# Loads of q, k and v moved from GpSimd's DMA queue to SyncE's, with the casts, the tails and the order of work changed along

## The chip, the cores and the metric

The kernel runs on one core of one Trainium2 chip. The metric is the device time of one execution in microseconds. A core has TensorE (PE, with its weight loads as PEld), VectorE (DVE), ScalarE (ACT), GpSimd (POOL) and SyncE (SP), and 16 DMA engines[...].

## What is computed

Linear attention with a feature map, then a two-layer block on its output. Batch and heads are 8 and 8, a sequence has 576 positions, a head 64 elements; the inner width is 2048.

```python
def phi(x):
    proj = np.einsum('bhsd,df->bhsf', x, w_phi)              # 64 -> 128
    proj = proj - np.max(np.abs(proj), axis=-1, keepdims=True)
    return np.concatenate([np.exp(proj), np.exp(-proj)], axis=-1)
q_p, k_p = phi(q), phi(k)
kv  = np.einsum('bhsf,bhsd->bhfd', k_p, v)
z   = np.sum(k_p, axis=2)
num = np.einsum('bhsf,bhfd->bhsd', q_p, kv)
den = np.einsum('bhsf,bhf->bhs', q_p, z)[..., None] + 1e-06
x   = (num / den), heads side by side: 4608 tokens x 512
h = x @ w_in                                                 # 512 -> 2048
g = np.where(h > 0, h, np.exp(np.minimum(h, 0)) - 1)
out = g @ w_out                                              # 2048 -> 512
```

## The kernel before

Attention works on quads: four heads of one batch, so 16 quads. Of 576 positions of a head, 512 are the main part (four rows of 128, `NT`), 64 the tail. The tails of the four heads are packed into one tile of 128 partitions: heads 0 and 2 on partitions 0 to 63, heads 1 and 3 on 64 to 127 (s is the half, c the pair).

Steps of a quad, each a function in `attention_steps`:

- `transposes`: TensorE transposes k and q (L166, tails L174), DVE copies them from PSUM to `kT`, `qT`.
- `k_head` (four heads and the tail): a projection `pk` (L195), a reduction for the largest absolute value `m_k` on DVE (L202), two exponentials `EK` on ACT (L215).
- `k_scale`: `em` on ACT (L223), then POOL scales v by it into `vs` (L229) and, for the tails, into `vst` (L240), a tile with zeros for the other half.
- `q_head`: projection and reduction `m_q`. `q_features`: projection `pq` (L250) and exponentials `Eq` (L258), tails `Eqt` (L273), and `w` (L280).
- `kv`: TensorE sums `EK` times `vs` (L299) and the tails (L288) into `pkv`; ACT copies it to `kv`.
- `out_head` and `out_tail`: `Eq` times `kv` gives `pn` (L322, tails L344), DVE weights and adds them into `tot` and `tott`; column 64 is the denominator.
- `divide`: `den` and `rec` on DVE (L367, L372, L373), `x` on POOL (L376, tails `xt` L382).
- `x_out`: TensorE transposes `x` (L393), DVE copies it into `xT` of its batch, and the tails into `xT_tail`.

The second block (called MoE in the code) works on chunks of 512 tokens: eight chunks of main rows, one per batch, and one of all tails. `mm1` is one of 16 first-stage units of a chunk: four matmuls `ph` (L438), `e_sb` on ACT (L446), `u_sb` on POOL (L448), `gT` on DVE (L451). `mm2` is one of four second-stage units: 16 matmuls `po` (L459), a copy `o_sb` on ACT (L467), a DMA out. 180 units in all. Their PSUM tiles come from a pool of four, those of attention from another four.

The loop over n runs 17 slots. Slot n does kv, out and x of quad n-1 mixed with k, scale and q of quad n, and the transposes of quad n+1 at its end. After slots 2, 4, ... the units of the batch just finished are put into `pending`, and the next two slots put them between their steps: none in slots 0 to 2, eight per slot in 3 and 4, ten per slot from 5 to 16; 44 are left for the end.

Loads: k and q of a quad by POOL's software queue with a cast to bf16 (L136), tails of a whole batch by six DMAs on the same queue (L108), weights and w_phi there too (L84, L91, L72, L73); v in fp32 by SP (L145), where the outputs are issued as well (L470). [...]the framework that builds the program may hoist an instruction ahead of others of its queue where its inputs allow. [...]

Of the kernel before, what the change touches and what calls it, by code (L numbers as in the profile page):

```python
# [12 lines left out]
ACT = mybir.ActivationFunctionType  # L13

# [7 lines left out]
def kernel(  # L22
# [11 lines left out]
    P = 128  # L34
# [11 lines left out]
    N_CHUNK = NTOK // CHUNK  # L46
    NT = 4
    MAIN = NT * P
    TAIL = S - MAIN
    NQ = 2 * B  # L50
    D1 = D + 1

    consts = ctx.enter_context(tc.tile_pool(name="consts", bufs=1))
    loads = ctx.enter_context(tc.tile_pool(name="loads", bufs=3))
    work = ctx.enter_context(tc.tile_pool(name="work", bufs=2))
    small = ctx.enter_context(tc.tile_pool(name="small", bufs=4))
    xtp = ctx.enter_context(tc.tile_pool(name="xtp", bufs=3))
# [10 lines left out]
    make_identity(nc, ident)  # L68

    w_phi_both = consts.tile([P, 2, F], BF16)  # L70
    nc.vector.memset(w_phi_both, 0.0)
    nc.gpsimd.dma_start(out=w_phi_both[0:D, 0, :], in_=w_phi)  # L72
    nc.gpsimd.dma_start(out=w_phi_both[D:P, 1, :], in_=w_phi)  # L73
# [7 lines left out]
    def load_w_in():  # L81
        for ct in range(N_CT):
            for c in range(2):
                nc.gpsimd.dma_start(  # L84
                    out=w_in_sb[c * D:(c + 1) * D, ct, :],
                    in_=w_in_r[ct // 2, c, ct % 2],
                )

    def load_w_out():
        for jt in range(0, N_JT, 4):  # L90
            nc.gpsimd.dma_start(  # L91
                out=w_out_sb[:, jt:jt + 4, :], in_=w_out_r[:, jt:jt + 4, :]
            )
# [5 lines left out]
    q_tails = consts.tile([P, NQ, 2, D], BF16)  # L99
    k_tails = consts.tile([P, NQ, 2, D], BF16)  # L100
    v_tails = consts.tile([P, NQ, 2, D1], BF16)
    nc.vector.memset(v_tails[:, :, :, D:D1], 1.0)

    def load_tails(b):
        for src, dst in ((k, k_tails), (q, q_tails), (v, v_tails)):
            heads = src[b].rearrange("(gc s) j d -> s j gc d", s=2)
            for s in range(2):
                nc.gpsimd.dma_start(  # L108
                    out=dst[s * TAIL:(s + 1) * TAIL, 2 * b:2 * b + 2, :, 0:D].rearrange(
                        "p g c d -> p (g c) d"  # L110
                    ),
                    in_=heads[s, MAIN:S],
                )


    NV = 3
    v_bufs = []
    for i in range(NV):
        vb = consts.tile([P, 4, NT, D1], FP32, name=f"v_main{i}")
        nc.vector.memset(vb[:, :, :, D:D1], 1.0)  # L120
        v_bufs.append(vb)

    vst_bufs = []
    for i in range(2):
        t = consts.tile([P, 2, 2, 2, D1], BF16, name=f"vst{i}")
        nc.vector.memset(t, 0.0)
        vst_bufs.append(t)

    qk_loaded = {}

    def load_quad(i):
        b, qd = divmod(i, 2)
        got = []
        for src, nm in ((k, "k_main"), (q, "q_main")):
            t = loads.tile([P, 4, NT * D], BF16, name=nm)
            nc.gpsimd.dma_start(  # L136
                out=t,
                in_=src[b, 4 * qd:4 * qd + 4, 0:MAIN, :].rearrange(
                    "h (p t) d -> p h (t d)", t=NT
                ),  # L140
            )
            got.append(t)
        vb = v_bufs[i % NV]
        for hh in range(4):
            nc.sync.dma_start(  # L145
                out=vb[:, hh, :, 0:D],
                in_=v[b, 4 * qd + hh, 0:MAIN, :].rearrange(
                    "(p t) d -> p t d", t=NT
                ),
            )  # L150
        qk_loaded[i] = (got[0], got[1], vb)


    def attention_steps(i):
# [3 lines left out]
        def transposes():  # L158
            k_main, q_main, _ = qk_loaded[i]
            kT = work.tile([P, 9, P], BF16, name="kT")  # L160
            qT = work.tile([P, 9, P], BF16, name="qT")
            for src, dst in ((k_main, kT), (q_main, qT)):
                tr = apsum.tile([P, 8, P], BF16, name="tr", tag="ap")
                for hh in range(4):
                    for tp in range(2):
                        nc.tensor.transpose(  # L166
                            tr[:, 2 * hh + tp, :],
                            src[:, hh, tp * P:(tp + 1) * P],
                            ident,
                        )  # L170
                nc.vector.tensor_copy(dst[:, 0:8, :], tr)  # L171
            trt = apsum.tile([P, 2, P], BF16, name="trt", tag="ap")
            for n, (src, dst) in enumerate(((k_tails, kT), (q_tails, qT))):
                nc.tensor.transpose(  # L174
                    trt[:, n, :],
                    src[:, i, :, :].rearrange("p c d -> p (c d)"),
                    ident,
                )
            nc.vector.tensor_copy(kT[:, 8, :], trt[:, 0, :])
            nc.vector.tensor_copy(qT[:, 8, :], trt[:, 1, :])  # L180
            st["kT"], st["qT"] = kT, qT
            st["m_k"] = small.tile([P, 18], FP32, name="m_k")
            st["m_q"] = small.tile([P, 18], FP32, name="m_q")
            st["EK"] = work.tile([P, 4, 2, NT * F], BF16, name="EK")
            st["EKt"] = work.tile([P, 2, 2 * F], BF16, name="EKt")
            st["Eq"] = work.tile([P, 2, 2, 2, 4 * P], BF16, name="Eq")
            st["Eqt"] = work.tile([P, 2, 2 * P], BF16, name="Eqt")

        def project(xT, hh, m):
# [4 lines left out]
            for j in range(n):  # L194
                nc.tensor.matmul(  # L195
                    pk[:, 2 * j:2 * j + 2, :].rearrange("p a b -> p (a b)"),
                    xT[:, 2 * hh + j, :],
                    w_phi_rhs,
                    start=True,
                    stop=True,  # L200
                )
            nc.vector.tensor_reduce(  # L202
                m[:, 4 * hh:4 * hh + 2 * n],
# [16 lines left out]
        def k_scale():  # L220
            em = small.tile([P, 2, 18], FP32, name="em")
            for sg in range(2):
                nc.scalar.activation(  # L223
                    em[:, sg, :], st["m_k"], ACT.Exp, scale=2.0 * sg - 1.0
                )
            vb = qk_loaded[i][2]
            vs = work.tile([P, 4, 2, NT, D1], BF16, name="vs")
            for hh in range(4):
                nc.gpsimd.tensor_tensor(  # L229
                    vs[:, hh],  # L230
                    vb[:, hh:hh + 1].to_broadcast((P, 2, NT, D1)),
                    em[:, :, 4 * hh:4 * hh + 4, None].to_broadcast(
                        (P, 2, NT, D1)
                    ),
                    op=ALU.mult,
                )
            vst = vst_bufs[i % 2]
            for s in range(2):
                r = slice(s * TAIL, (s + 1) * TAIL)
                nc.gpsimd.tensor_tensor(  # L240
                    vst[r, :, :, s, :],
                    v_tails[r, i:i + 1].to_broadcast((TAIL, 2, 2, D1)),
                    em[r, :, 16:18, None].to_broadcast((TAIL, 2, 2, D1)),
                    op=ALU.mult,
                )
            st["vs"], st["vst"] = vs, vst
# [15 lines left out]
        def q_features_tail():  # L262
# [16 lines left out]
            w = small.tile([P, 18], FP32, name="w")  # L279
# [3 lines left out]
        def kv(c):  # L283
            if c == 0:
                st["kv"] = work.tile([P, 2, 2, 2, D1], BF16, name="kv")
            pkv = apsum.tile([P, 2, 2, D1], FP32, name="pkv", tag="ap")
            for sg in range(2):
                nc.tensor.matmul(  # L288
                    pkv[:, :, sg, :],
                    st["EKt"][:, sg, c * F:(c + 1) * F],  # L290
                    st["vst"][:, sg, c, :, :],
                    start=(sg == 0),
                    stop=False,
                    skip_group_check=True,
                )
            for s in range(2):
                for sg in range(2):
                    for t in range(NT):
                        nc.tensor.matmul(  # L299
                            pkv[:, s, sg, :],  # L300
                            st["EK"][:, 2 * c + s, sg, t * F:(t + 1) * F],
                            st["vs"][:, 2 * c + s, sg, t, :],
                            start=False,
                            stop=(t == NT - 1),
                            skip_group_check=True,
                        )
            nc.scalar.copy(st["kv"][:, c], pkv)

        def out_head(hh):
            c, s = divmod(hh, 2)  # L310
            if hh == 0:
                st["tot"] = work.tile([P, 4, NT, D1], FP32, name="tot", bufs=1)
                st["tott"] = work.tile([P, 2, D1], FP32, name="tott")
                st["x"] = work.tile([P, 2, NT, 2, D], BF16, name="x")
                st["xt"] = work.tile([P, 2, D], BF16, name="xt")
            pn = []
            for sg in range(2):
                pt = apsum.tile([P, NT, D1], FP32, name=f"pn{sg}", tag="ap")
                for t in range(NT):
# [5 lines left out]
                        st["kv"][:, c, s, sg, :],  # L325
# [4 lines left out]
            tot = st["tot"][:, hh]  # L330
# [3 lines left out]
                st["w"][:, 4 * hh:4 * hh + 4, None].to_broadcast((P, NT, D1)),  # L334
# [4 lines left out]
        def out_tail():  # L339
            pn = []  # L340
            for sg in range(2):
                pt = apsum.tile([P, 2, 2, D1], FP32, name=f"pn{sg}", tag="ap")
# [245 lines left out]
```

## Time and profile before

| | |
|---|---|
| median of 3 runs | 508.6 us (507.23 to 509.34) |
| the profiled execution | 507.1 us, span 505.3 us, mean granted clock 0.922 |
| PE busy | 409.6 us (81%) |
| PEld | 223.1 us (44%) |
| DVE | 306.1 us (61%) |
| ACT | 268.3 us (53%) |
| POOL | 278.5 us (55%), DMA issues counted in |
| DMA | 32.55 MB, mean 64 GB/s; software queue 14.19 MB, hardware queue 17.83 MB |
| chain that ended last | PE 52%, POOL 20%, DVE 13%, DMA 6% |

Busy time is a sum over the span; the stages differ, so the views by time below count for more. The span is what the profile sees, the execution's own time 1.8 us more. Rows of groups read: line, engine, operation, output and inputs, shapes, count, then busy us and mean ns of one, then idle time of the engine before them and who ended it.

### The profile page before, as it was taken

Reading aid. Unit: us, or ns where it says so; the run is one execution under the profiler, and the core shown is the slowest. Engines: PE = TensorE matmul, PEld = TensorE weight load, DVE = VectorE, ACT = ScalarE, POOL = GpSimd, SP = SyncE. Lnnn points to the kernel's source line nnn. Section 1 sums busy time; section 2 is a strip of 40 time slices with the busy share of each in tenths; the row PEclk is TensorE's granted clock in tenths of the full one; section 3 lists DMA queues with packets and bytes.
Section 4 is the critical chain, followed back from the end, with each engine's and each line's share of the span. In section 5 each row is a group of like instructions: output and inputs, shape, how many; then the busy total and the mean of one; then the engine's idle time right before and its main releaser. Section 6 shows DMA issues by size and latency. Waiting matters only on the chain.

```text
span 505.3 us, 8410 instructions
## 1 busy us (share of the span) xinstructions
PE 409.6 (81%) x3070; PEld 223.1 (44%) x3120; DVE 306.1 (61%) x647; ACT 268.3 (53%) x581; POOL 278.5 (55%) x420
## 2 busy tenths in 40 slices
PE   2573727495979797979797979797979798999996
PEld 1251415252635364536363546354545354444442
DVE  2562826886857677766777577757775855334420
ACT  1742608292847474847484748474847462444431
POOL 8669799747473737373737383818281734333310
PEclk9965959797989899989999999999998999899999
DMA  9999948231323232324242424200000000110113
GB/s 157 212 181 198 116 61 76 47 43 43 44 63 64 62 64 64 64 64 64 64 64 62 64 65 64 62 22 21 22 23 23 21 22 22 42 43 21 43 52 72
DMA packets 71944, 32.55 MB, mean 64 GB/s; under 512 B 48352, under 2 KB 66784, under 8 KB 71904
## 3 DMA queue, kind: packets, MB, share of 16 engines
q0 software_dynamic: 32864, 14.19, 23.1%
q1 hardware_dynamic: 39040, 17.83, 13.2%
q8 instruction: 24, 0.39, 0.3%
q14 instruction: 16, 0.13, 0.1%
HBM read 36.77 MB, written 9.44 MB: 91 GB/s over the span
## 4 chain that ended last, share of the span: by engine, by line
PE 52%; POOL 20%; DVE 13%; DMA 6%; issue 4%; ACT 4%; POOLq 0%; ACTq 0%
PE po L459 22%; PE ph L438 13%; POOL x L376 7%; DMA q_main<-in_q_dram 5%; POOL vs L229 4%; DVE m_q L202 4%; PE pq L250 4%; PE pn L322 3%; PE pkv L299 2%; POOL vst L240 2%; PE pk L195 2%; ACT EK L215 2%; POOL u_sb L448 2%; PE tr L166 2%; DVE den L367 2%
## 5 line engine op out<-in xcount | busy, mean ns | idle before, releaser
L448 POOL TENSOR_SCALAR u_sb<-e_sb 128x512 bf16<-128x512 f32 x144 | 88.9, 623 | 134.9 <-ACT e_sb L446 129.5
L459 PE MATMUL po<-w_out_sb,gT 128*128 128x512 bf16 x559 | 148.1, 389 | 1.8 <-DVE gT L451 1.4
L451 DVE SCALAR_TENSOR_TENSOR gT<-u_sb,ph 128x512 bf16<-128x512 bf16 x144 | 97.9, 683 | 78.9 <-POOL u_sb L448 78.1
L438 PE MATMUL ph<-xT,w_in_sb 128*128 128x512 bf16 x480 | 131.0, 390 | 4.6 <-DVE gT L451 3.4
L446 ACT ACTIVATE e_sb<-ph 128x512 f32<-128x512 f32 x144 | 87.3, 611 | 48.8 <-PE ph L438 46.8
L258 ACT ACTIVATE Eq<-pq 128x512 bf16<-128x512 f32 x128 | 65.2, 616 | 54.7 <-PE pq L250 54.7
L459 PEld LDWEIGHTS <-gT 128*128 128x128 bf16 x576 | 54.4, 100 | 50.5 <-issue 4.6
L438 PEld LDWEIGHTS <-w_in_sb 128*128 128x128 bf16 x576 | 54.6, 100 | 49.6 <-issue 6.8
L215 ACT ACTIVATE EK<-pk 128x512 bf16<-128x512 f32 x128 | 69.4, 612 | 13.1 <-DVE m_k L202 13.0
L229 POOL TENSOR_TENSOR vs<-v_main,em 128x520 bf16<-128x520 f32 x64 | 65.7, 1063 | 17.9 <-ACT em L223 17.7
L202 DVE TENSOR_REDUCE m_k<-pk 128x4 f32<-128x512 f32 (+1 forms) x80 | 50.4, 632 | 25.9 <-PE pk L195 25.6
L467 ACT COPY o_sb<-po 128x512 f32<-128x512 f32 x36 | 21.2, 589 | 68.0 <-PE po L459 67.5
L393 PE MATMUL tr<-ident,x 128*128 128x128 bf16 x128 | 14.6, 248 | 52.7 <-POOL x L376 52.7
L202 DVE TENSOR_REDUCE m_q<-pk 128x4 f32<-128x512 f32 (+1 forms) x80 | 48.5, 628 | 1.3 <-PE pk L195 0.5
L322 PEld LDWEIGHTS <-Eq 128*128 128x128 bf16 x512 | 28.9, 98 | 24.9 <-issue 17.0
L376 POOL TENSOR_TENSOR x<-tot,rec 128x256 bf16<-128x256 f32 x64 | 37.2, 614 | 3.1 <-DVE rec L373 3.0
L393 PEld LDWEIGHTS <-x 128*128 128x128 bf16 x128 | 8.4, 108 | 68.8 <-POOL x L376 68.8
L322 PE MATMUL pn<-kv,Eq 128*128 128x65 bf16 x512 | 34.0, 194 | 3.8 <-ACT EK L215 2.6
L195 PE MATMUL pk<-w_phi_both,qT 128*128 128x256 bf16 x144 | 29.6, 292 | 8.4 <-DVE m_q L202 7.0
L136 POOL DMA_DIRECT2D k_main<-in_k_dram x16 | 12.8, 802 | 35.9 <-PE tr L166 25.3
L195 PE MATMUL pk<-w_phi_both,kT 128*128 128x256 bf16 x144 | 29.6, 284 | 3.3 <-ACT EK L215 1.0
L171 DVE COPY kT<-tr 128x1024 bf16<-128x1024 bf16 x16 | 11.1, 692 | 34.1 <-PE tr L166 34.1
(61 smaller groups left out, 462.2 us busy)
## 6 DMA issues: line engine op xcount, KB each, us to landing
v_main<-in_v_dram SPq DMA_DIRECT2D x64, 128.0 KB, 3.3
out_dram<-o_sb SPq DMA_DIRECT2D x32, 256.0 KB, 2.6
k_main<-in_k_dram POOLq DMA_DIRECT2D x16, 256.0 KB, 5.3
q_main<-in_q_dram POOLq DMA_DIRECT2D x16, 256.0 KB, 5.7
w_in_sb<-in_moe_w_in_dram POOLq DMA_DIRECT2D x8, 256.0 KB, 10.2
w_out_sb<-in_moe_w_out_dram POOLq DMA_DIRECT2D x4, 512.0 KB, 8.3
out_dram<-o_sb SPq DMA_DIRECT2D x8, 128.0 KB, 2.3
k_tails<-in_k_dram POOLq DMA_DIRECT2D x16, 32.0 KB, 2.8
```

Source lines behind the costliest of these rows:

```text
L195: nc.tensor.matmul(pk[:, 2 * j:2 * j + 2, :].rearrange("p a b -> p (a b)"), xT[:, 2 * hh + j, :], w_phi_rhs, start=True, stop=True,)
L202: nc.vector.tensor_reduce(m[:, 4 * hh:4 * hh + 2 * n], pk[:, 0:2 * n, :], axis=AX.X, op=ALU.max, apply_absolute_value=True,)
L215: nc.scalar.activation(dst, pk, ACT.Exp, scale=1.0 - 2.0 * sg)
L229: nc.gpsimd.tensor_tensor(vs[:, hh], vb[:, hh:hh + 1].to_broadcast((P, 2, NT, D1)), em[:, :, 4 * hh:4 * hh + 4, None].to_broadcast((P, 2, ...
L258: nc.scalar.activation(st["Eq"][:, par, c, sg, :], pq, ACT.Exp, scale=1.0 - 2.0 * sg)
L322: nc.tensor.matmul(pt[:, t, :], st["Eq"][:, par, c, sg, o:o + P], st["kv"][:, c, s, sg, :], start=True, stop=True,)
L376: nc.gpsimd.tensor_tensor(st["x"][:, s, :, c, :], st["tot"][:, hh, :, 0:D], rec[:, 4 * hh:4 * hh + 4, None].to_broadcast((P, NT, D)), op=A ...
L438: nc.tensor.matmul(ph, w_in_sb[:, ct, jt * P:(jt + 1) * P], xTs[ch][:, ct, :], start=(ct == 0), stop=(ct == N_CT - 1),)
L446: nc.scalar.activation(e_sb, ph, ACT.Exp)
L448: nc.gpsimd.tensor_scalar(u_sb, e_sb, -1.0, 1.0, op0=ALU.add, op1=ALU.mult)
L451: nc.vector.scalar_tensor_tensor(gTs[ch][:, jt, :], u_sb, 0.0, ph, op0=ALU.min, op1=ALU.max)
L459: nc.tensor.matmul(po, gT[:, jt, tt * P:(tt + 1) * P], w_out_sb[:, jt, :], start=(jt == 0), stop=(jt == N_JT - 1),)
```

## The change

- k, q and v, tails included, are loaded by SP in fp32: four DMAs for k, four for q, six for v per quad. k and q land in staging tiles of 1152 columns (`k_st`, `q_st`, two of each), the last 128 columns hold the tails. POOL casts each in two pieces into `k_bf`, `q_bf`.
- Each quad's positions are nine columns per pair c (eight of two heads and one of tails), so `vs`, `tot`, `x`, `m`, `w`, `den` hold main part and tails in one tile; `vst`, `tott`, `xt` are gone. `vs` is four POOL instructions of 585 elements, `x` two of 576.
- The tail's matmuls read only their own 64 rows (`kv`: 64 rows of weights and of `vs`) or write only their own 64 (`out_tail`: 64 columns of weights). `kv(s)` takes the heads of one half s instead of a pair c.
- POOL's software queue carries weights alone, one issue after every second step of slots 0 and 1, `w_out` in eight DMAs for four. w_phi comes by SP and is cast by DVE.
- Slot 2 does kv, out and x of quad 1 first, then the keys and queries of quad 2. From there units are placed by an even rate, 136 of them over 14.4 slots; a second-stage unit follows after four first-stage ones. x comes after three q heads instead of five; scale comes after the tail's out and divide.
- `o_sb` has two buffers for four, `xT` two for three.

The core of the diff:

```diff
-        for src, nm in ((k, "k_main"), (q, "q_main")):
-            t = loads.tile([P, 4, NT * D], BF16, name=nm)
-            nc.gpsimd.dma_start(out=t, in_=...)
+        for src, nm in ((k, "k_st"), (q, "q_st")):
+            t = stage.tile([P, QW + P], FP32, name=nm)
+            heads = src[b, 4 * qd:4 * qd + 4]
+            for hh in range(0, 4, 2):
+                nc.sync.dma_start(out=t[:, hh * NT * D:(hh + 2) * NT * D]..., in_=heads[hh:hh + 2, 0:MAIN, :]...)
+            for s in range(2):
+                nc.sync.dma_start(out=t[s * TAIL:(s + 1) * TAIL, QW:]..., in_=...[s, MAIN:S])
...
+        def cast(n):
+            nm = ("k_bf", "q_bf")[n]
+            t = st[nm] = work.tile([P, QW + P], BF16, name=nm)
+            src = loaded[i][n]
+            for lo, hi in ((0, QW // 2), (QW // 2, QW + P)):
+                nc.gpsimd.tensor_copy(t[:, lo:hi], src[:, lo:hi])
...
+            for c in range(2):
+                for sg in range(2):
+                    r = slice(c * NS, (c + 1) * NS)
+                    nc.gpsimd.tensor_tensor(vs[:, sg, r, :], vb[:, r, :], em[:, sg, r, None]..., op=ALU.mult)
...
+            r = slice(s * TAIL, (s + 1) * TAIL)
+            for c in range(2):
+                for sg in range(2):
+                    nc.tensor.matmul(pkv[:, c, sg, :], st["EKt"][r, sg, c * F:(c + 1) * F],
+                                     st["vs"][r, sg, c * NS + 8, :], start=False, ...)
...
+                        o = c * P + s * TAIL
+                        nc.tensor.matmul(pt[r, sg, c, :], st["Eqt"][:, sg, o:o + TAIL], st["kv"][:, s, c, sg, :], ...)
...
+        if nxt:
+            steps += nxt["cast"]
+        if n == 2:
+            steps += old["kv"] + old["out"] + old["x"]
+            steps.append(lambda: chunk_ready(0))
+            steps += new["k"] + new["scale"] + new["q"] + new["qf"] + nxt["tr"]
+            return steps
...
+            if weights and n < 2 and j % 2 == 1:
+                weights.pop(0)()
+            due = (n + (j + 1) / len(steps) - 2.6) * 136 / 14.4
+            while done < due and (first or second):
+                moe_unit()
+                done += 1
...
+        if n + 2 < NQ:
+            load_qk(n + 2)
+            load_v(n + 2)
```

## The prediction, made before the changed kernel ran

> **What bounds the kernel now.** I read the slices of the page first (each digit is the busy tenth of 12.6 us):
>
> ```profile
> PE   2573727495979797979797979797979798999996
> ...
> POOL 8669799747473737373737383818281734333310
> PEclk9965959797989899989999999999998999899999
> DMA  9999948231323232324242424200000000110113
> ```
>
> The first twelve slices (152 us) differ from the rest: TensorE is mostly idle, POOL (GpSimd) is nearly full, its granted clock (PEclk) dips with the idle stretches, and the DMA engines are full for five slices only. The timeline of POOL alone shows with what:
>
> ```profile
> 56.65 1.23 POOL L108 DMA_DIRECT2D k_tails<-in_k_dram  x2
> 57.85 1.26 POOL L108 DMA_DIRECT2D q_tails<-in_q_dram  x2
> 59.06 1.28 POOL L108 DMA_DIRECT2D v_tails<-in_v_dram  x2
> 60.26 1.30 POOL L108 DMA_DIRECT2D k_tails<-in_k_dram  x2
> 61.82 1.24 POOL L108 DMA_DIRECT2D q_tails<-in_q_dram  x2 [0.26 <-issue]
> 63.03 1.25 POOL L108 DMA_DIRECT2D v_tails<-in_v_dram  x2
> ...
> 64.86 4.14 POOL L229 TENSOR_TENSOR vs<-v_main,em 128x520 bf16<-128x520 f32 x4
> 68.92 1.36 POOL L240 TENSOR_TENSOR vst<-v_tails,em 64x260 bf16<-64x260 bf16 x2
> ...
> 70.96 2.32 POOL L376 TENSOR_TENSOR x<-tot,rec 128x256 bf16<-128x256 f32 x4
> ```
>
> From 56.65 to 64.86 POOL only issues DMAs of tails, most for later batches, while the keys of quad 2 wait to be scaled: `vs` of that quad starts at 64.86 and `x` of quad 1 at 70.96. TensorE needs this `x` to start the first MoE chunk. So POOL's queue, not TensorE, sets the first 97 us. Later, the table by windows (time, then busy us of PE, PEld, DVE, ACT, POOL, then granted clock, DMA share, GB/s) shows one stretch of about a slot per line:
>
> ```profile
> 76.00:101.00 25.00, 15.59 (x143) 9.30 (x145) 19.31 (x37) 13.63 (x34) 21.71 (x34) 0.84 0.56 61
> 101.00:126.00 25.00, 18.01 (x155) 10.27 (x157) 18.83 (x42) 14.56 (x35) 14.36 (x21) 0.85 0.27 43
> ...
> 202.00:227.00 25.00, 22.24 (x180) 12.23 (x181) 18.23 (x39) 15.62 (x35) 14.40 (x21) 0.96 0.31 64
> ```
>
> A slot with ten MoE units takes 25.6 us (x to x: from 169.95 to 426.15 in ten slots), one with eight 24.1 (120.46 to 144.58). By matmul pitch (0.2157 us for 512 columns, from 3.45 us for 16 in the chain of waits) the same slots need 20.8 and 17.5 us. So a slot is not TensorE's alone: 3.3 us more matmul costs 1.5 us. What fills the difference is in the waits (us in total, times, longest) and the groups:
>
> ```profile
> POOL u_sb L448 <- ACT e_sb L446: 129.5, 88, 5.1
> ...
> PE tr L393 <- POOL x L376: 52.7, 27, 9.7
> ```
>
> ```profile
> L448 POOL TENSOR_SCALAR u_sb<-e_sb 128x512 bf16<-128x512 f32 x144 | 88.9, 623 | 134.9 <-ACT e_sb L446 129.5 <-DVE tot L331 3.9
> ...
> L229 POOL TENSOR_TENSOR vs<-v_main,em 128x520 bf16<-128x520 f32 x64 | 65.7, 1063 | 17.9 <-ACT em L223 17.7
> ...
> L376 POOL TENSOR_TENSOR x<-tot,rec 128x256 bf16<-128x256 f32 x64 | 37.2, 614 | 3.1 <-DVE rec L373 3.0
> ...
> L108 POOL DMA_DIRECT2D k_tails<-in_k_dram x16 | 10.2, 654 | 0.0
> ```
>
> After the em of a slot, POOL runs vs (4.1), vst (1.3), one or two u_sb (0.62 each) and x (2.3) in this order, about 8.3 us, and PE waits for x at the end of it, 2.4 us per slot in the steady part.
>
> [...]
>
> **The change part by part**, for the profiled execution (span 505.3, its run 507.1; so I add 1.8 to a span, and 1.5 more for the median of 508.6).
>
> *POOL.* Removed: k, q and w_phi issues 12.8 + 12.1 + 1.1, tails 30.5, vst 19.9, xt 6.4. vs becomes 64 of 585 elements at 2.04 ns, 1.20 each, 76.5 (was 65.7); x 32 of 576, by the two rows 614 for 256 and 397 for 128 (1.70 ns each + 180) 1.16 each, 37.0 (was 37.2). Added: 64 casts, 512 or 640 fp32 to bf16, by L448 0.62 and 0.78, 2.8 per quad, 44.9[...]; w_out in 8 issues for 4, +2.4. Sum 278.5 to about 254; per slot the part from em to x falls from 8.3 to 4.8 + 0.6 + 2.3 = 7.7.
>
> *SP.* 14 loads per quad for 4, at 0.54 us (L145's shortest): 7.6 us of a slot, no bound. [...]outputs stand behind them, but land in 2.6 us and are read by nobody. Loads of quad i+2 wait for the cast of quad i, two slots ahead of their own cast, so in the steady part casts find data. DMA engines: k and q are written in fp32, 2 x 4.7 MB more; hidden later (share 0.3), not in the first 60 us.
>
> *Start.* (1) Quad 0's loads issue from SP in 8 x 0.54 and land by 7.5, w_phi by 8.5; two small DVE copies (0.21 each, by L179) make it bf16: the first projection at 9 for 11.5. (2) Quad 1's loads wait behind v(0) until about 10 and land at 16; POOL's casts of quad 1 stand ahead of vs(0), so vs(0) runs 18 to 23 for 20.97 to 26.3: 3 us gained of what the issues cost. (3) In slot 1 x(0) comes after the last w_out issues[...]: x(0) at 36 for 44.6, vs(1) until 43. (4) Slot 2 does batch 0's kv, out and x first: 43 + 9 = 52 by durations; the casts of quads 3 and 4 stand ahead of x(1) on POOL and need 5 quads and all weights, 12.5 MB written; the kernel before moved at most 212 GB/s, so 59 if nothing gets faster with fp32 rows, 52 if it does. I take 57, for 70.96. (5) Slot 2's keys now come after x instead of beside: + 8.5 to em, + 4.8 vs: kv(2) at 70 for 79.5. So x(2) is at 86 for 96.84. **Start: -10.5** (-17 to 0).
>
> *Slots x(2) to x(15).* 329.3 us for 13 now. By instruction order the matmuls there fall from 259 to 257 us, since 136 units are spread evenly instead of eight then ten: by the slope of one half -1. The part from em to x -0.6 per slot, DVE's tail work (tott, two den) -0.8 beside others, taken as -0.2. x stands two q heads earlier in PE's order: 3.7 us of matmul cover it after the tail for 5.0, so PE idles longer, but the moved work fills the stretch before the next kv, which is TensorE's: 0. Casts follow x, while ACT is in its 4.03 us of Eq and u_sb waits for e_sb anyway (129.5 us of such waits): 0; their cost uncovered is the rival below. [...] Eight more small matmuls per quad (65 columns, 0.0325 each) replace eight of 130 at 0.06: 0. Sum 13 x (-0.8 + 0.3) - 1 = **-7.5** (-20 to +12).
>
> *End.* 44 units stand after the last slot in both, 318 matmuls after the last x for 323: **-1**. o_sb's two buffers: outputs are 3.45 us apart and land in 2.6: 0 (at most 0.5 each over four). xT's two: chunk b-2 is through its first matmul by then: 0.
>
> Sum: 505.3 - 10.5 - 7.5 - 1 + 1.8 = 488 beside the profiled run's 507.1; with the median's 1.5, about **489**.
>
> **Rivals.** *R1, start only*: slots keep 25.3 us[...]: 508.6 - 11.5 = 497. For it: slots are partly TensorE's. Against: POOL's stretch is shorter. *R2, slower: casts ahead of u_sb.* POOL would hold x and casts, 5.1 us, then vs, with few u_sb between; four PSUM buffers hold four first-stage units, and PE stops when their u_sb is late. If all 2.8 us show in each of 13 slots, 36 us on top of 489: 526; three quarters, 517. It decides from 1.5 us per slot (19.5 of 13 slots eat the whole gain). Against it: 7.7 us per slot of POOL waiting for e_sb. *R3, DMA is the start's bound*: the doubled k and q bytes delay casts and weights, x(2) stays at 97: 500 with the slots' gain, 508 without.
>
> **How the numbers follow.** Main case 0.48 (478 to 496), R1 0.22, R2 0.21, R3 0.09. A measurement here tells 0.5% (2.5 us) from no change. Faster: main, R1 and a small part of R3, 0.72; same: most of R3, 0.07; slower: R2, 0.21. Range: 469 (start at -17 and slots at -20 leave it just below) to 517 (R2 to its middle).
>
> **What would show it.** Right: no L108-like issues on POOL, x(1) before 62, x(2) near 86, slots near 24.8, casts beside Eq. Wrong: POOL casts waiting for DMA; u_sb waits on casts with PE ph waiting for gT[...].

## The result, and the profile after

The changed kernel takes **515.9 us** (median of 4 runs, 515.3 to 518.3) beside 509.0 for the kernel before in the same runs: a ratio of **1.014, 95% interval 1.010 to 1.018**. It is slower; the forecast was 489, faster. The profiled execution has a span of 516.5 us for 505.3, and a mean granted clock of 0.904 for 0.922.

The slices of the changed kernel's page, each digit a fortieth of the span (12.9 us). Line numbers in what follows are those of each kernel's own code.

```profile
PE   3574468599959797788979797979796979899996
...
POOL 3549345725573535564446556444444262533320
PEclk9855777889988999898979899989897989999999
DMA  6999866233322322142323232120000001011103
```

POOL is less busy in the first eight slices than it was, as forecast. But TensorE's clock shows a 7 or 8 in eight of the slices 17 to 33; before it did so in one. POOL's timeline after the start (start, duration, instruction, idle time before it and who ended it) shows what stands where the tails' DMA issues stood:

```profile
58.84 0.62 POOL L152 CAST k_bf<-k_st 128x512 bf16<-128x512 f32 x1 [4.28 <-DMA k_st<-in_k_dram]
...
62.78 0.72 POOL L152 CAST q_bf<-q_st 128x640 bf16<-128x640 f32 x1 [1.02 <-DMA q_st<-in_q_dram]
63.46 2.26 POOL L348 TENSOR_TENSOR x<-tot,rec 128x576 bf16<-128x576 f32 x2
73.11 2.28 POOL L217 TENSOR_TENSOR vs<-v_main,em 128x585 bf16<-128x585 f32 x2 [7.40 <-ACT em L209]
```

x of quad 1, x(1) for short, starts at 63.46 for 70.96: 7.5 us earlier, though four casts that wait for their loads stand ahead of it. The keys of quad 2 now come after it, `vs` only at 73.11, and x(2) is at 98.72 for 96.84: the gain is gone within one slot. From x(2) to x(15) it takes 341.3 us for 329.3. The end, last x to end of span, takes 76.5 for 79.1. The table by windows, over two slots each (time, then busy us of PE, PEld, DVE, ACT, POOL, then granted clock, DMA share, GB/s):

```profile
150.90:206.90 56.00, 46.10 (x376) 25.95 (x382) 32.38 (x70) 29.77 (x68) 26.29 (x35) 0.91 0.29 82
...
258.80:310.90 52.10, 44.68 (x367) 24.94 (x374) 33.97 (x72) 30.22 (x69) 28.13 (x37) 0.90 0.30 84
```

The waits (us in total, times, longest) and the groups (busy us, mean ns of one, idle time before them and who ended it) that answer to those of before:

```profile
POOL u_sb L414 <- ACT e_sb L412: 142.1, 75, 8.9
...
PE tr L358 <- POOL x L348: 63.2, 15, 8.8
...
POOL k_bf L152 <- PE trt L163: 38.5, 10, 7.1
```

```profile
L217 POOL TENSOR_TENSOR vs<-v_main,em 128x585 bf16<-128x585 f32 x64 | 72.5, 1167 | 31.5 <-ACT em L209 31.3
...
L348 POOL TENSOR_TENSOR x<-tot,rec 128x576 bf16<-128x576 f32 x32 | 36.2, 1153 | 0.0
```

The prices of POOL's work came out as worked out (`vs` 1.17 us for 1.20, x 1.15 for 1.16, a pair of casts 1.33 for 1.40; POOL 245.9 us in all for 254). So the time was not lost in the size of POOL's new instructions. What grew is TensorE's wait for x, 63.2 us for 52.7.

### The profile page after: what moved, and what is told of

The parts are those of the page before. It is cut to its first block, busy times and chain, and to the rows that moved or that the text cites. A ratio compares the mean times of both kernels' runs of the same rounds, so it can differ in the third digit from the quotient of the medians.

```text
span 516.5 us, 8710 instructions
## 1 busy us (share of the span) xinstructions
PE 417.9 (81%) x3195; PEld 231.1 (45%) x3248; DVE 286.0 (55%) x598; ACT 263.4 (51%) x581; POOL 245.9 (48%) x326
## 4 chain that ended last, share of the span: by engine, by line
PE 36%; POOL 22%; issue 16%; DVE 5%; ACT 4%; POOLq 0%; ACTq 0%
PE po L425 17%; PE ph L404 11%; POOL vs L217 9%; POOL x L348 6%; POOL u_sb L414 5%; DVE gT L417 2%; PE pn L300 2%; PE pk L180 2%; ACT EK L201 2%; POOL q_bf L152 2%; ACT e_sb L412 1%; DVE m_k L188 1%; PE pkv L267 1%; PE tr L358 1%; PE pq L226 1%
## 5 line engine op out<-in xcount | busy, mean ns | idle before, releaser
L404 PE MATMUL ph<-xT,w_in_sb 128*128 128x512 bf16 x483 | 140.4, 399 | 5.5 <-DVE gT L417 3.0
L425 PE MATMUL po<-w_out_sb,gT 128*128 128x512 bf16 x553 | 141.3, 391 | 1.5 <-issue 0.5
L217 POOL TENSOR_TENSOR vs<-v_main,em 128x585 bf16<-128x585 f32 x64 | 72.5, 1167 | 31.5 <-ACT em L209 31.3
L425 PEld LDWEIGHTS <-gT 128*128 128x128 bf16 x576 | 55.7, 100 | 58.9 <-issue 7.0
L404 PEld LDWEIGHTS <-w_in_sb 128*128 128x128 bf16 x576 | 54.6, 102 | 52.3 <-issue 15.1
L358 PE MATMUL tr<-ident,x 128*128 128x128 bf16 x128 | 13.6, 271 | 63.2 <-POOL x L348 63.2
L188 DVE TENSOR_REDUCE m_k<-pk 128x4 f32<-128x512 f32 (+1 forms) x80 | 50.0, 632 | 18.2 <-PE pk L180 18.0
L152 POOL CAST k_bf<-k_st 128x512 bf16<-128x512 f32 (+1 forms) x32 | 20.8, 667 | 58.5 <-PE trt L163 38.5
L358 PEld LDWEIGHTS <-x 128*128 128x128 bf16 x128 | 10.2, 122 | 70.4 <-POOL x L348 70.2
L365 DVE COPY xT<-tr 128x1024 bf16<-128x1024 bf16 x16 | 11.0, 689 | 47.0 <-PE tr L358 47.0
L348 POOL TENSOR_TENSOR x<-tot,rec 128x576 bf16<-128x576 f32 x32 | 36.2, 1153 | 0.0
L300 PE MATMUL pn<-kv,Eq 128*128 128x65 bf16 x512 | 32.8, 196 | 2.9 <-ACT EK L201 0.8
L310 DVE TENSOR_TENSOR tot<-pn,w 128x260 f32<-128x260 f32 x64 | 27.0, 423 | 9.1 <-PE pn L300 7.7
```

The lines of the kernel that those rows point to most:

```text
L188: nc.vector.tensor_reduce(m[:, o:o + NT] if hh < 4 else m[:, NS - 1::NS], pk[:, 0:2 * n, :], axis=AX.X, op=ALU.max, apply_absolute_value=True,
L217: nc.gpsimd.tensor_tensor(vs[:, sg, r, :], vb[:, r, :], em[:, sg, r, None].to_broadcast((P, NS, D1)), op=ALU.mult,)
L300: nc.tensor.matmul(pt[:, t, :], st["Eq"][:, par, c, sg, o:o + P], st["kv"][:, s, c, sg, :], start=True, stop=True,)
L348: nc.gpsimd.tensor_tensor(st["x"][:, :, c, :], st["tot"][:, r, 0:D], rec[:, r, None].to_broadcast((P, NS, D)), op=ALU.mult,)
L404: nc.tensor.matmul(ph, w_in_sb[:, ct, jt * P:(jt + 1) * P], xTs[ch][:, ct, :], start=(ct == 0), stop=(ct == N_CT - 1),)
L425: nc.tensor.matmul(po, gT[:, jt, tt * P:(tt + 1) * P], w_out_sb[:, jt, :], start=(jt == 0), stop=(jt == N_JT - 1),)
```

## The experiments

Three theories. **A, the order**: loads, casts and joined tails gain as forecast, and what costs is the new order of work (slot 2's branch, the even rate of units, the place of x and scale). **B, the casts**: they hold POOL's queue, as in the rival R2. **C, the 64-row matmuls**: they cost TensorE time where they stand beside 128-row ones. That was the author's assumption; every matmul of the kernel before is `128*128`, so its trace does not show it. Times are medians, ratios to the kernel before in the same runs; where a difference between two other kernels is given, it is that of medians of runs that may lie in different sessions.

### The order put back, and the rivals

*The old order*: slot 2's branch out, steps and units as before; loads, casts and tails as changed. (The edits are shortened here and below.)

```diff
-        if n == 2: (kv, out, x of quad 1 first)
-            steps += old["out"][3:]              # then scale, q[:3], x, q[3:]
+            steps += [old["out"][3], new["scale"][0], old["out"][4]]   # then q, x
-            due = (n + (j + 1) / len(steps) - 2.6) * 136 / 14.4
+            upto = share * (j + 1) // len(steps)
```

> The changed kernel with the order of work of the kernel before: slot 2 mixes quad 1 and quad 2 like any other slot, units stand where the kernel before puts them (none in slots 0 to 2, eight, then ten a slot, one second-stage unit after each four of the first stage), x after all five q heads, scale before the tail's out. Loads by SP in fp32, casts on POOL, the joined tails and the 64-row matmuls stay. Theory A (the order costs, the rest gains): 493 to 501 us, faster than both; x(2) by 93, slots x(2) to x(15) 322 us in sum or less (the kernel before 329, the changed one 341). Theory B (the casts on POOL cost: they hold the queue while k_bf's buffer is taken or the load is late): 511 to 517, near the changed kernel, with slots above 329. Theory C[...]: also 511 to 517, but then without tail at 64 rows it gets faster.

**492.3 us, 0.968 (0.963 to 0.974).** x(1) 67.1, x(2) 90.4, slots x(2) to x(15) 316.7. These are theory A's numbers, the time 0.7 us below its range: the new loads, casts and tails are worth some 16 us, and the new order costs 24, more than all of it.

*Three buffers for the casts' tiles*:

```diff
-            t = st[nm] = work.tile([P, QW + P], BF16, name=nm)
+            t = st[nm] = work.tile([P, QW + P], BF16, name=nm, bufs=3)
```

> The changed kernel with three buffers each for k_bf and q_bf instead of two, so that a cast no longer waits for TensorE's transposes of two quads before (38.5 us of POOL's waits). Theory B: 4 to 12 us faster than the changed kernel (504 to 512), with the wait of k_bf for PE gone and x earlier in its slot. Theory A: within 2 us of the changed kernel (514 to 518), as POOL's queue waits there for u_sb's e_sb instead.

516.6 us, 1.016 (1.012 to 1.019): no gain. But the wait that this was to take away is still there, 31.0 us in 9 waits for 38.5 in 10, so the run by itself doesn't test B; what that wait is for stays open. The old order does: it keeps the casts, with 29.3 us of the same wait, and gains all the same. B is out as the main cause.

*The tail's matmuls at full size*:

```diff
-            r = slice(s * TAIL, (s + 1) * TAIL)
+            r = slice(0, P)
```

> The changed kernel with the tail's matmuls at full size (128 rows of weights and vs in kv, 128 columns of weights in the tail's out), same number: no change of matmul size is left. It adds the other half's tails into each sum, so it computes something else than the reference. Theory C: 4 us or more faster[...], 508 to 512. Theories A and B: within 2 us of the changed kernel (514 to 518).

(In the tail's out, the columns of the weights are widened likewise.) 514.9 us, 1.012 (1.006 to 1.019), no difference from 1.014 that these runs can tell. The answers by tile, changed kernel and then this one, give the tail's matmul the same median, 193 ns:

```profile
L279 PE MATMUL pkv<-vs,EKt x128: 188/193/243, 27.5 to 429.2; 64*128 64x65 bf16 x128
```

```profile
L279 PE MATMUL pkv<-vs,EKt x128: 191/193/247, 27.4 to 426.6; 128*128 128x65 bf16 x128
```

The three numbers are minimum, median and maximum in ns. C is out.

*k and q by POOL's queue again*, on the old order, in bf16 and without casts:

```diff
-            t = stage.tile([P, QW + P], FP32, name=nm)
-                nc.sync.dma_start(...)                       # 8 a quad, then 4 casts
+            t = stage.tile([P, QW + P], BF16, name=nm)
+            nc.gpsimd.dma_start(out=t[:, 0:QW]..., in_=heads[:, 0:MAIN, :]...)   # 6 a quad
```

> The old order of steps and units (492.3) with k and q loaded by POOL's software queue in bf16 again, six issues a quad in place of four casts; v stays with SP, the joined tails and 64-row matmuls stay. POOL pays 6 x 0.65 to 0.78 = 4.2 us a quad for 2.8 us of casts. If the gain of 15.7 us lies in the joined tails (vs, x, and no tail copies in advance): 491 to 498. If it lies in the loads (POOL free of issues in the first 60 us): 499 to 506, with x(1) at 70 and x(2) at 95.

492.9 us, 0.970 (0.966 to 0.974), the same as the old order's 492.3. Between these two ways of loading k and q, by SP with casts on POOL or by POOL's queue without them, there is no difference here. What is left of the gain, joined tails, 64-row matmuls, no tails loaded in advance, the weights' issues spread over slots 0 and 1, v's tails and w_phi by SP, was not split further.

### The order taken apart

*Slot 2 mixed again*, all else as changed (the `if n == 2` branch out):

> The changed kernel without its special slot 2 (quad 1's kv, out and x first, then quad 2): slot 2 is mixed as all others. Units keep the even rate. Theory A: x(1) later by some 3 to 6 us (67 to 70), since keys of quad 2 come in between, but x(2) earlier by 3 to 8 (91 to 96 for 98.7); the time 508 to 513. If the slots alone carry the loss (x(2) to x(15) stays at 341 and x(2) does not move), 515 to 517. Theory B: 514 to 518, since the casts of quad 3 wait as before.

510.5 us, 1.005 (1.002 to 1.007): the branch costs 5.4 us. x(2) is at 94.6 for 98.7; the slots stay (339.0).

*Of the two edits left, the units' old placement alone*:

> Between the old order (492.3) and the one without slot 2's branch (510.5) lie two edits; this kernel takes one of them back: units placed as in the kernel before, x after three q heads and scale after the tail's out as in the changed one. Theory A1 (the units' placement costs: the even rate, started at 2.6 slots, runs ahead of the first-stage units, and second-stage units of 16 matmuls follow one another with nothing of the first stage between, in front of x and the last heads): 491 to 497, slots x(2) to x(15) 315 to 320 us in sum. Theory A2 (x two q heads earlier, PE stands at its transposes): 504 to 511, slots above 330.

499.9 us, 0.985 (0.980 to 0.989): neither range. *The old steps with the even rate*:

> The other edit alone: the even rate of units with the old order of steps (x after five q heads, scale before the tail's out, slot 2 mixed). Theory A1: 504 to 511, slots of two lengths again (24 and 28 us or more), sum above 330. Theory A2: 491 to 497.

501.4 us, 0.988 (0.984 to 0.992): neither range again. So each edit costs by itself, 7.6 us the steps and 9.1 the units, and together 18.2. A1 and A2 are both half right.

*Only x moved* up by two heads, in the old order:

```diff
-            steps += new["q"]
+            steps += new["q"][:3]          # x, then new["q"][3:]
```

> The old order (492.3) with one step moved: x after three q heads instead of five; scale stays before the tail's out. If x's place is what cost 7.6 us in the order of steps: 497 to 502, with waits for x 0.5 to 1 us longer and more steps of lost clock than the old order's 11.9 us. If the later scale was it: 490 to 494.

502.8 us, 0.991 (0.988 to 0.994): 10.4 us for the place of x alone, 0.8 more than its range allows, so the later scale costs nothing more (both together were 7.6). The waits for x, which were to be 0.5 to 1 us longer each, are 0.1 longer (2.12 and 2.42 us for 2.01 and 2.31).

*The changed kernel with units from 3.0 slots on*:

> The changed kernel with one number changed: units begin at 3.0 slots instead of 2.6, so that first-stage units are still there when a batch's first quad is done, and second-stage units stand alone (no two in a row until slot 16). Three units more stay for the end. Theory A1: the slots of 28 us and more go, sum x(2) to x(15) 318 to 328 for 341, end 3 to 6 us longer, x(2) as before at 97 to 99: 500 to 507. Theory A2: 514 to 520, slots as they were.

512.6 us, 1.013 (1.007 to 1.019), slots 337.5, x(2) 5.4 us earlier and the end 3.9 longer: between the two ranges, and not told apart from the changed kernel. In the slots of the changed kernel there are three stretches of 61, 45 and 31 `po` matmuls with no `ph` between them, here none of 20 or more. So second-stage units in a row were not what made its rate costly.

### Where in the slot the order costs

Below are TensorE's and POOL's timelines in one slot of the changed kernel, from the tail's out to x:

```profile
200.97 0.33 PE L325 MATMUL pnt<-kv,Eqt 128*64 128x65 bf16 x8
201.23 0.82 PE L404 MATMUL ph<-xT,w_in_sb 128*128 128x512 bf16 x3
201.88 0.82 PE L180 MATMUL pk<-w_phi_both,qT 128*128 128x256 bf16 x6
202.54 1.46 PE L404 MATMUL ph<-xT,w_in_sb 128*128 128x512 bf16 x6
209.21 1.04 PE L358 MATMUL tr<-ident,x 128*128 128x128 bf16 x8 [5.21 <-POOL x L348]
```

```profile
201.82 4.53 POOL L217 TENSOR_TENSOR vs<-v_main,em 128x585 bf16<-128x585 f32 x4
206.31 0.62 POOL L414 TENSOR_SCALAR u_sb<-e_sb 128x512 bf16<-128x512 f32 x1
206.90 2.26 POOL L348 TENSOR_TENSOR x<-tot,rec 128x576 bf16<-128x576 f32 x2
```

And the same stretch of the old order, TensorE and then POOL:

```profile
257.16 0.33 PE L325 MATMUL pnt<-kv,Eqt 128*64 128x65 bf16 x8
257.42 1.04 PE L425 MATMUL po<-w_out_sb,gT 128*128 128x512 bf16 x4
258.51 0.82 PE L180 MATMUL pk<-w_phi_both,qT 128*128 128x256 bf16 x6
259.16 1.03 PE L404 MATMUL ph<-xT,w_in_sb 128*128 128x512 bf16 x4
260.02 0.49 PE L180 MATMUL pk<-w_phi_both,qT 128*128 128x256 bf16 x3
260.35 1.46 PE L404 MATMUL ph<-xT,w_in_sb 128*128 128x512 bf16 x6
264.12 0.62 PE L358 MATMUL tr<-ident,x 128*128 128x128 bf16 x8 [2.31 <-POOL x L348]
```

```profile
257.30 4.55 POOL L217 TENSOR_TENSOR vs<-v_main,em 128x585 bf16<-128x585 f32 x4 [1.69 <-ACT em L209]
261.81 2.25 POOL L348 TENSOR_TENSOR x<-tot,rec 128x576 bf16<-128x576 f32 x2
```

In both, x stands behind `vs` on POOL, and is done 8.2 and 6.9 us after the tail's out begins. In the old order TensorE has 4.4 us of other matmuls behind the tail and stands for 2.3; in the changed one it has 2.8 us and stands for 5.2. The rest of the difference is x itself, which is 1.3 us later: `vs` starts 0.8 us after the tail's out for 0.1, and a `u_sb` stands before x. This is the longest of the changed kernel's waits after x(2); they are 1.5 to 5.2 us, 3.6 on average, and 2.5 on average in the old order. What follows is the second part. The changed kernel by windows, across this wait:

```profile
206.00:208.00 2.00, 0.00 (x0) 0.00 (x0) 0.69 (x1) 0.00 (x0) 2.00 (x3) 1.00 0.44 100
208.00:209.00 1.00, 0.00 (x0) 0.00 (x0) 0.00 (x0) 0.00 (x0) 1.00 (x2) 1.00 0.88 200
209.00:210.00 1.00, 0.79 (x8) 0.80 (x9) 0.00 (x0) 0.00 (x0) 1.00 (x3) 0.52 0.46 102
210.00:211.00 1.00, 0.99 (x7) 0.75 (x6) 0.72 (x2) 0.00 (x0) 0.32 (x1) 0.50 0.05 11
211.00:212.00 1.00, 0.79 (x2) 0.30 (x2) 1.00 (x4) 0.00 (x0) 0.00 (x0) 0.50 0.00 0
212.00:213.00 1.00, 1.00 (x5) 0.43 (x4) 1.00 (x3) 0.26 (x1) 0.00 (x0) 0.77 0.00 0
213.00:214.00 1.00, 1.00 (x7) 0.41 (x6) 0.23 (x1) 1.00 (x3) 0.58 (x1) 1.00 0.00 0
```

When TensorE starts again, its clock (third number from the end) is 0.50 for 3.4 us; this is called a drop below. The time lost is one minus the clock, times the window: 0.48 + 0.50 + 0.50 + 0.23 = 1.71 us. The wait before it is 5.21 us long; a wait of 2.02 us was followed by a drop as well, at 237.06 in the old order (last section).

Summed over windows of 1 us from x(2) to x(15), both taken 3 us later so that the wait for x(2) is out and the one for x(15) in, with TensorE's idle time before x's transposes there, the slots divide so (us; the rest is the sum less the two). The slots are those of the one profiled run, whose time is given beside the median:

| kernel | median | profiled run | x(2) to x(15) | waits for x | lost clock | rest |
|---|---|---|---|---|---|---|
| before | 508.6 | 507.1 | 329.3 | 33.8 | 15.1 | 280.4 |
| changed | 515.9 | 518.3 | 341.3 | 42.7 | 25.0 | 273.6 |
| no slot 2 branch | 510.5 | 511.9 | 339.0 | 42.4 | 22.2 | 274.4 |
| even units, old steps | 501.4 | 498.8 | 327.9 | 30.2 | 22.9 | 274.8 |
| new steps, old units | 499.9 | 501.6 | 328.3 | 34.0 | 17.5 | 276.8 |
| x moved alone | 502.8 | 501.7 | 329.9 | 32.1 | 22.1 | 275.7 |
| old order | 492.3 | 488.8 | 316.7 | 32.6 | 10.3 | 273.8 |

For the changed loads and tails the rest is 273.6 to 276.8 in these six orders: the 24.6 us between the changed kernel's slots and the old order's are 10.1 us of waits and 14.7 of lost clock. Where x is moved alone the waits are no longer in sum (32.1), and 11.8 of 13.2 us are clock. That is an account from one profiled execution each, not yet a test. The old order's is the fastest of its four (488.8 us at a mean clock of 0.964; the others took 492.1 to 495.7 at 0.923 to 0.926), so its lost clock lies at the low end.

That lost clock costs time can be read inside the old order's trace. The slots from x(6) to x(7) and from x(8) to x(9) hold the same number of instructions on each engine, and TensorE waits 2.0 us for x in both. One has no drop in it, the other has one:

```profile
187.93:211.63 23.70, 21.31 (x189) 12.18 (x191) 17.38 (x38) 15.69 (x35) 13.44 (x18) 1.00 0.34 88
236.76:261.81 25.05, 22.50 (x189) 12.67 (x191) 17.38 (x38) 15.79 (x35) 13.44 (x18) 0.93 0.30 86
```

A drop of 1.71 us costs 1.35 here. Slots alike but for one drop differ by 1.1 to 1.4 us in three more traces (k and q by POOL's queue; x moved alone; new steps with old units). So the clock is a cost beside the wait, of two thirds to four fifths of what the column says where it can be compared (1.1 to 1.4 us for 1.71).

### A test that tested something else

*Work put into the wait*: transposes of a constant tile ahead of x's, in the changed kernel and in the old order.

```diff
             tr = apsum.tile([P, 8, P], BF16, name="tr", tag="ap")
+            for j in range(32):                     # 24 in the old order
+                nc.tensor.transpose(tr[:, j % 8, :], ident, ident)
```

> The changed kernel with work added: 32 transposes of the constant identity tile into x's own PSUM tile ahead of x's transposes, so that TensorE is busy for about 1.8 us of each wait for x (13 waits of 3.6 us on average after the third). They are overwritten and change no result. Theory K (each long wait for x lets the granted clock fall to half for 1.7 to 3.4 us of lost work; from 75 us on the changed kernel lost 29 us so, in steps of 1.71): the steps of lost clock after 75 us fall to a third or less, and the time to 496 to 507 although work is added. Theory W (only the waiting counts, the clock is a by-product): 514 to 519, as the waits end when x comes.

> The changed kernel's loads, casts and tails with the old order (492.3), and 24 such transposes ahead of x's: about 1.35 us of each wait for x of 2.0 to 2.3 us. Theory K: the 11.9 us of lost clock from 75 us on fall to 3 to 6: 483 to 489. Theory W: 491 to 495.

532.3 us, 1.049 (1.045 to 1.053), and 506.9, 0.998 (0.996 to 1.000): 16 and 15 us slower, outside every range. The old order's timeline of TensorE shows why:

```profile
265.26 1.50 PE L358 MATMUL tr<-ident 128*128 128x128 bf16 x24
269.03 0.62 PE L360 MATMUL tr<-ident,x 128*128 128x128 bf16 x8 [2.27 <-POOL x L348]
```

The transposes stand where in the old order six `ph` matmuls stand (260.35 in its fence above), and the wait after them is as long as it was: the framework that orders the queue had already put matmuls into that wait, and put these in their place. Waits (29.3 us) and lost clock (11.8) stay near the old order's, and the rest grows by 19.3 us, about 13 times the 1.50 us of the transposes. These two runs say nothing about the clock. *With units spread from a batch's x on* as well:

> The one before with units of a batch spread from its x on instead of from the end of that slot, at 20 units over 54 steps (16 for the first batch): some seven units come earlier into slot 2, where TensorE has room, and as many fewer stand in slot 16. If the room in slot 2 is free, 3 to 8 us under the one before (478 to 486); if x(2) gets later by what is put in, no change.

522.7 us, 1.029 (1.024 to 1.034): slower by another 16, where 3 to 8 us less or no change was expected. x(2) moves by 1.6 us only, the slots grow to 352.2.

### The wait taken away

*x on VectorE*, so that it no longer stands behind `vs`, in the changed kernel and in the old order:

```diff
-                nc.gpsimd.tensor_tensor(st["x"][:, :, c, :], ...)
+                nc.vector.tensor_tensor(st["x"][:, :, c, :], ...)
```

> The changed kernel with x's two multiplications on VectorE instead of POOL. x then no longer stands behind the four vs (4.6 us) on POOL's queue. Theory X (the order costs by the wait for x and by the clock that falls after it: 47 us of waits and 26 us of lost clock after x(2)): waits for x under 1 us each, lost clock after 90 us under 12 us, time 465 to 490. Theory Y (the units' and heads' order costs TensorE by itself): 500 to 514. If VectorE becomes late instead[...]: 510 to 525.

> The old order (492.3) with x on VectorE. Waits for x after x(2) 35.5 us, lost clock 12 us: 455 to 475. Theory X: within 8 us of the changed kernel with the same edit, since the wait that told the two apart is gone. Theory Y: 15 us or more below it. If VectorE becomes late: 488 to 500.

**478.2 us, 0.941 (0.938 to 0.945), and 471.7, 0.927 (0.925 to 0.929).** One line makes the changed kernel 37.7 us faster and the old order 20.6, and of the 23.6 us between the two 6.5 are left: theory X, and a version that beats both kernels. In the slots of the changed kernel waits fall from 42.7 to 20.1 and lost clock from 25.0 to 8.4; in the old order from 32.6 to 18.9 and from 10.3 to 4.6. The waits were to fall below 1 us each in the changed kernel, and are still about 1.8, and 1.5 in the old order. The waits of the changed kernel with x on VectorE:

```profile
PEld L358 <- DVE x L348: 38.5, 15, 5.2
...
PE tr L358 <- DVE x L348: 31.5, 14, 4.8
```

The 39.2 us that waits and clock give back in the changed kernel's slots become 29.8 there (341.3 to 311.5), as the rest grows by 9.4 (283.0; in the old order by 8.0); what TensorE meets there instead was not followed. x(2) comes 10.9 us earlier too. The edit also takes 36.2 us of work off POOL. In the slots the rest, where such a gain would show, rises instead; in the start the two were not told apart.

*Without slot 2's branch as well*, and *the kernel before with x on VectorE*:

> The changed kernel with x on VectorE (478.2) and without slot 2's branch. If the branch is the rest of the difference to the old order: 471 to 475. If the units' and heads' order is: 476 to 480, x(2) earlier and the slots as long as before (311 us).

> The kernel before with its five multiplications into x and xt on VectorE. Its waits for x after x(2) are 33 us and its lost clock after 90 us 19 us. If the wait for x is what it pays there too: 480 to 492. If VectorE, which has more to do there (306 us), becomes late: 500 to 512. The joined tails and loads keep their gain if it stays 10 us or more above 471.7.

477.5 us, 0.938 (0.934 to 0.942): the branch now costs nothing that can be told (x(2) 2.8 us earlier, the slots 3.3 longer), so by subtraction the 6 us left are units and steps. And 497.2, 0.976 (0.972 to 0.981), some 5 us over the range: before pays for the wait too, but only 11.5 us; the new loads and tails are worth 25 us beside it.

*Two tries to go further from 471.7*, units spread from x on, and three buffers for the casts:

> The one before with units of a batch spread from its x on (20 units over 54 steps, 16 for the first batch) instead of from the end of that slot. If slot 2 has room on TensorE: 3 to 8 us below the one before. If the units pushed into it hold x(2) back, as in the run with added transposes: 5 us or more above.

> The old order with x on VectorE and three buffers each for k_bf and q_bf. Once x is off POOL, casts that wait for a buffer could be what holds u_sb: then 3 us or more below the one with two buffers; else within 2 us of it.

495.1 us, 0.973 (0.971 to 0.976), and 473.3, 0.931 (0.928 to 0.933). The second changes nothing that can be told. The first loses 23 us: waits for x are 30.9 for 18.9 and lost clock 18.5 for 4.6, so this placement, too, pays in those two terms. x(2) is not held back (83.3 us for 85.0). Why later waits are longer was not found.

## Why the prediction was wrong

**What bounds the kernel: right.** POOL's queue in the start, and x behind `vs` in the slots. Taking x off POOL is what pays most. (The slices were read loosely: TensorE is busy for more than half of the first twelve, not mostly idle, and POOL is at six tenths or more only in the first eight throughout.) But the 2.4 us of wait per slot were taken as a given cost of the slot, not as the thing that the order decides.

**POOL's sum, the tails, the loads: right in sum.** With the order put back, the start gains 6.5 us for 10.5 and the slots 12.6 for 7.5 in the profiled run of 488.8 us, where the sum said 488 for a profiled run; the median is 492.3 for 489. That the two parts missed in opposite ways is luck, and some of the slots' gain is clock (10.3 us lost for 15.1), which the sum did not have. Two sizes were off. x(1) was put at 57, between 52 and 59, and came at 63.5, since the casts ahead of it waited for their loads: R3's mechanism, in part. And the +0.3 us per slot in the sum, the author's estimate of what 64-row matmuls beside 128-row ones would cost, did not show: 514.9 us with all of them at full size for 515.9.

**The step that failed: "x stands two q heads earlier in PE's order ... so PE idles longer, but the moved work fills the stretch before the next kv, which is TensorE's: 0."** The idling was seen and priced at nothing. The place of x alone costs 10.4 us in the old order. There the waits hardly grow (32.1 us in sum for 32.6), and what the profiled slots lose is clock, 22.1 us for 10.3. Part of that may be chance (8 of 10 waits near 2 us brought a drop in one trace, 2 of 10 in the other; last section), but the runs lie apart: 501.6 to 504.7 us for 488.8 to 495.7. With the even rate beside it the waits grow too, to 42.7 us for 32.6, and the rest (273.6 for 273.8) shows no work moved behind them that won it back. So a term was missing from the sum altogether: the clock after the wait, which the page shows as PEclk, and which had been read only as a mark of the idle start.

**Even spread of units, -1: wrong.** 9.1 us slower; in the profiled slots the waits are no longer in sum (30.2 us for 32.6), and the lost clock is 22.9 for 10.3. From x(3) on five waits last 3.4 to 4.8 us, each with a drop after it, where the old order has two above 2.5. The term counted matmuls, by the slope of one half between slots with eight and with ten, and not what stands beside the wait for x.

**Slot 2, quad 1 first: wrong.** x(1) came earlier, but the keys of quad 2 cost more than it gave: kv(2) at 82.6 for the 70 forecast (79.5 before), and 5.4 us in the run.

**The end, -1: about right**, 2.6 us shorter. What was priced at nothing for the casts held: in the old order the time is the same with them and without.

**The rivals.** R2 named 517 as the slow outcome (three quarters of 36 us on 489 are 516), and the time fell on it for another reason: the casts were not it (492.3 us with them, 492.9 without, in the old order). The slow rival that was needed, a longer wait for x in each slot with its clock, was not among them, and that the range holds the result, by R2's end, is luck.

## What to carry to other kernels

Where one engine waits for another at a fixed place of each iteration, work out what the order puts into that wait before moving the place: cover that is lost can cost its length, and here it cost TensorE's clock after the wait as well (1.35 us for one drop of 1.71). If the wait stands behind another job in a queue, taking it off that queue can be worth more than any reordering (37.7 us here, for 23.6 by the order). And filler added to a program whose builder orders the queue can take the place of work that was there (15 us slower here): look at the order in the trace before reading the time.

## What the runs showed of the hardware

- **Lost clock came in steps of 1.71 us** (3.41 us at half clock), one or two after a wait, at times three. In each of the twenty traces the stretches at half clock began whole multiples of 3.41 us apart, at other times in each execution. With the time divided at these points into windows of 3.41 us, and counted after 85 us, a window at full clock in which TensorE was busy for less than 0.4 was followed by half clock in 129 of 129 cases, between 0.4 and 0.5 in 26 of 54, and above in 1 of 1997; a window at half clock was followed by full clock in 153 of 154 cases when busy for more than 0.8, and in 0 of 45 when under 0.7. So two waits of the same length came out differently: in the old order one of 2.01 us at 287.24 falls into two windows, and one of 2.02 at 237.06 into one (TensorE alone: busy us, granted clock, DMA):

```profile
284.24:287.65 3.41, 3.00 (x17) 1.00 0.47 137
287.65:291.06 3.41, 1.75 (x14) 1.00 0.50 113
291.06:294.48 3.42, 3.41 (x30) 1.00 0.00 0
...
236.45:239.86 3.41, 1.39 (x14) 1.00 0.61 143
239.86:243.28 3.42, 3.20 (x10) 0.50 0.01 2
```

- **Longer waits were followed by a drop more often.** In nine of these traces (before, changed, and the seven with x on POOL that alter order, rate or loads) idle time before x's transposes after 85 us came with a drop (from its start to 6 us after its end) in 37 of 39 cases above 3.5 us (mean loss 2.6 us), in 9 of 13 between 2.5 and 3.5, and in 29 of 56 between 1.9 and 2.5 (mean loss 0.9).
- **The mean clock of a whole run tells little of its time.** In 54 executions of the kernel before it lies between 0.912 and 0.944, some 16 us of clock, and the time (506.1 to 511.7 us) hardly goes with it, 0.03 us per us lost. The drops in the slots cost time, as shown above (1.35 us for one of 1.71); why the time goes so little with the mean was not found.
- **x on VectorE takes 0.75 us when POOL computes nothing (25 instructions), 1.16 beside `u_sb` (39), and 1.3 to 1.7 beside `vs` (57)**, in the five kernels with the joined tails. So it was stretched, as `den` was in the kernel before (L367: 0.18 us with nothing on POOL, at 36.65; beside `vs` 0.57 to 0.70 in 11 of 13 cases, 0.18 and 3.68 in the other two), and the move paid nevertheless: 37.7 and 20.6 us.
- **64-row matmuls beside 128-row ones cost nothing measurable here**: 514.9 us with full-size ones for 515.9, and 193 ns for each of the two forms of `kv`'s tail.
